# Two weight loads on ScalarE's DMA queue, one joined store at the end, and last outputs in the buffers of x

## The chip, the cores and the metric

The kernel runs on one core of a Trainium2 chip. The core has five engines that work beside each other, each through its own list of instructions in order: TensorE (PE, matrix products and transposes into PSUM), VectorE (DVE), ScalarE (ACT), GpSimd (POOL) and SyncE (SP), which here only issues transfers. Sixteen DMA engines move data between HBM and SBUF for all of them. A transfer that is issued on SyncE stands in SyncE's queue, one that is issued on ScalarE in ScalarE's queue. The metric is the device time of one execution in microseconds (us).

## What is computed

A gated linear recurrence over 6336 steps for 4 sequences of 256 channels, and a highway layer on its result:

```python
sig = 1.0 / (1.0 + np.exp(-f_logit))
f = lower_bound + (1.0 - lower_bound) * sig
i = 1.0 - f
for t in range(S):
    h = f[:, t] * h + i[:, t] * x[:, t]
    y[:, t] = h
...
H = np.maximum(y @ w_h, 0.0)
T = 1.0 / (1.0 + np.exp(-(y @ w_t + b_t)))
out = T * H + (1.0 - T) * y
```

`x` and `f_logit` are 26 MB each in float32, the output 26 MB, `w_h` and `w_t` 256 x 256 float32, 256 KB each.

## The kernel before

The 25344 rows (4 sequences of 6336) are cut into 21 units of 2 to 16 blocks of 128 rows (`parts`, line 43). The first two units and the last have 2 blocks, those in the middle 16 (two loads of 8). For a unit n the steps are, by their letters in the order table:

- l and x load logits and x (line 260, issued on SP), 8 KB for each partition in a full load; u is the sigmoid on ScalarE (272); b multiplies u and x, on GpSimd or VectorE (287).
- i and p transpose u and b into PSUM on TensorE (296, 321), so that channels lie on partitions and time runs along the row; f makes the decay from u on ScalarE or VectorE (311, 309).
- s is the recurrence, one scan instruction on VectorE for each half of the channels (330).
- z and g are the products with w_t and w_h on TensorE (343 and, for the same weights again, 148); t is the sigmoid of z on ScalarE (366), d the max on VectorE (373), e the product of d and t on GpSimd or VectorE (387).
- o adds y and e and transposes back to rows on TensorE (404, 405); c copies the result from PSUM to an SBUF buffer, on ScalarE (416) or VectorE (414); w stores that buffer (422, issued on SP).

Around the start stand once-only steps. `wh` and `wt` load the two weights into `w_raw` (207, 204). `WI` subtracts the identity from w_h on GpSimd (230). `WH` and `WT` scale the weights by one minus the lower bound into `w_sb`: WHv on VectorE (235), WT on ScalarE (237). The two parameter vectors `prm` of 1 KB each are loaded on ScalarE's queue (170, 171). k is a number of dummy matmuls on TensorE.

The order of all this work is written out by hand in the string `order` (lines 50 to 112). A token is a letter with unit, chunk and part, then the number of the buffer or PSUM bank after a colon, and a v at its name where VectorE takes the step instead of the engine named first. Each engine runs its instructions in the order of the tokens. What stands behind an instruction on its engine waits for it. Buffers are named by letter and number: `c20.0.1:3` writes into buffer o3, and waits until the store that last read o3 has ended. The last unit, number 20, has two blocks and is stored in two parts of one block each, so it has `o20.0.0`, `o20.0.1`, `c20.0.0v`, `c20.0.1`, `w20.0.0` and `w20.0.1`.

Of the kernel before, what the change touches and what calls it, by code (L numbers as in the profile page):

```python
# [11 lines left out]
FP32 = mybir.dt.float32  # L12
# [7 lines left out]
def kernel(  # L20
# [10 lines left out]
    nc = tc.nc  # L31
    B, S, D = x.shape
    assert (B, S, D) == (4, 6336, 256)
    P = 128
    NH = D // P
    NB = 8
# [3 lines left out]


    CHUNK, GROUP = {17: 4, 18: 4}, {17: 2, 18: 2, 19: 2, 20: 1}
    parts = [(2,), (2,), (4,), (8,), (8,), (8,), (8,), (8, 8), (8, 8), (8, 8), (8, 8), (8, 8), (8, 8), (8, 8), (8,), (8,), (8,), (8,), (8,), (4,), (2,)]
    units, at = [], 0
    for subs in parts:
# [2 lines left out]
    assert at == B * S  # L48

    order = """  # L50
k*4:0 l1.0:0 u1.0:0 i1.0.0:0 i1.0.1:1 l0.0:1 x0.0:0 x1.0:1 u0.0:1 b0.0.0:0 pc:2 wh i0.0.0:3 i0.0.1:4 WI k*1:5 cc
p0.0.0:2 p0.0.1:5 k*16:6 l2.0:2 u2.0:2 wt b1.0.0:1 p1.0.1:6 f1.0:0 dgv f0.0v:1 f0.1v:2 s0.1:0 x2.0:2 WHv s0.0:1
g0.0.1:0 p1.0.0:2 b2.0.1v:2 g0.0.0:3 WT z0.0.0:4 i2.0.1:5 f1.1:3 s1.1:2 z0.0.1:1 i2.0.0:6 d0.0.0:0 d0.0.1 b2.0.0
l3.0:3 f2.1v:1 k*4:7 p2.0.0:0 p2.0.1:3 s1.0:3 x3.0:3 z1.0.1:2 z1.0.0:5 g1.0.1:7 l4.0:4 t0.0.0:0 f2.0:2 t0.0.1 k*4:1
g1.0.0:1 e0.0.1 x4.0:4 u3.0:3 s2.0:4 i3.0.0:0 k*4:4 t1.0.0:1 t1.0.1 s2.1:5 g2.0.0:2 d1.0.1:1 b3.0.0:0 d1.0.0 d2.0.0:2
# [48 lines left out]
s18.1:3 c16.0.0:2 g17.0.1:0 i19.0.1:1 f19.1:1 b19.0.0 p19.0.1:2 d17.0.1:3 d17.0.0 z18.1.0:3 E17.1 e17.0.1 g18.1.0:4  # L104
o17.1.0:0 o17.1.1:1 z18.1.1:5 t18.1.0:2 d18.1.0:1 e18.1.0 g18.1.1:3 g18.0.1:4 z18.0.1:6 c17.1.0:1 w16.0.1 w16.0.0
s19.1:0 p19.0.0:0 w17.1.0 c17.1.1:0 e17.0.0v w17.1.1 t18.1.1 t18.0.1:0 o17.0.1:1 c17.0.1:3 d18.1.1 e18.1.1 s19.0:1
o17.0.0:2 c17.0.0:2 p20.0.1:3 z18.0.0:5 d18.0.1:0 t18.0.0 g18.0.0:1 o18.1.0:0 d18.0.0 c18.1.0:1 e18.0.1 w17.0.0
p20.0.0:2 s20.1:4 z19.0.0:4 t19.0.0:1 g19.0.0:5 e18.0.0 i20.0.0:0 f20.0:3 o18.1.1:1 c18.1.1:0 z19.0.1:3 d19.0.0:2
g19.0.1:0 t19.0.1 o18.0.1:4 c18.0.1:2 s20.0:5 z20.0.1:1 t20.0.1:2 e19.0.0 o18.0.0:2 w17.0.1 d19.0.1 w18.1.0 e19.0.1v
z20.0.0:0 t20.0.0 w18.1.1 c18.0.0v:3 g20.0.0:3 d20.0.0:3 w18.0.1 w18.0.0 o19.0.0:4 c19.0.0:1 w19.0.0 g20.0.1:1 d20.0.1  # L110
e20.0.0v o19.0.1:0 c19.0.1:0 w19.0.1 e20.0.1v o20.0.0:1 c20.0.0v:2 w20.0.0 o20.0.1:0 c20.0.1:3 w20.0.1
"""

    pool = ctx.enter_context(tc.tile_pool(name="sb", bufs=1))
# [3 lines left out]
    st = [dict() for _ in units]  # L118
    once = {}
    pin = tc.keep_in_program_order  # L120

    def sb(shape, dtype, name, slot=0):
        return pool.tile(shape, dtype, tag=f"{name}{slot}", name=name)
# [48 lines left out]
    cc = sb([P, NH], FP32, "cc")  # L172
    ncc = sb([P, NH], FP32, "ncc")
    bt = sb([P, NH], FP32, "bt")
    w_raw = sb([P, 2, NH, D], FP32, "w_raw")
# [12 lines left out]
    def chunk(n, q):  # L188

        nb, c = sum(units[n][1]), CHUNK.get(n, NB)  # L190
        return q * c, min(c, nb - q * c)
# [9 lines left out]
                mybir.DependencyClass.Sync, mybir.DependencyReason.DATA), reason="shared port")  # L201

    def do_wt(slot, eng):
        pin(nc.sync.dma_start(w_raw[:, 1], moe_w_t.rearrange("(h p) o -> p h o", p=P)))

    def do_wh(slot, eng):
        pin(nc.sync.dma_start(w_raw[:, 0], moe_w_h.rearrange("(h p) o -> p h o", p=P)))

    def do_pc(slot, eng):
        once["prmT"] = Banks(slot).one(0)[:, :2 * NH]  # L210
# [42 lines left out]
    def rows(full, at, j0, j1):  # L253
        return full[at + j0 * P:at + j1 * P, :].rearrange("(p j) d -> p j d", p=P)
# [104 lines left out]
    def half(n, q, name, h):  # L359
        M = chunk(n, q)[1] * P  # L360
        return st[n][name, q][:, h * M:(h + 1) * M]
# [27 lines left out]
    def blocks(n, q, r):  # L389
        c0, cl = chunk(n, q)  # L390
        g = GROUP.get(n, 4)
        return c0 + r * g, c0 + min(r * g + g, cl)

    def do_o(eng, slot, n, q, r):
        op = Banks(slot)
        j0, j1 = blocks(n, q, r)
        c0 = chunk(n, q)[0]
        g = j1 - j0
        for j in range(g):
            whole = slice(j0 * P + j, j0 * P + j + g * (P - 1) + 1, g)  # L400
            cols = slice((j0 - c0) * P + j, (j0 - c0) * P + j + g * (P - 1) + 1, g)
            for h in range(NH):
                o = op.part(j * D + h * P, j * D + (h + 1) * P)
                pin(nc.tensor.matmul(o, st[n]["y", h][:, whole], diag[:, h], start=True, stop=False))  # L404
                pin(nc.tensor.matmul(o, half(n, q, "d", h)[:, cols], ident_b, start=False, stop=True))  # L405
        st[n]["op", q, r] = op

    def do_c(eng, slot, n, q, r):
        j0, j1 = blocks(n, q, r)
        o = sb([P, 4 * D], FP32, "o", slot)  # L410
        op = st[n]["op", q, r].all((j1 - j0) * D)
        to = o[:, :(j1 - j0) * D]
        if eng:
            pin(nc.vector.tensor_copy(to, op))
        else:
            pin(nc.scalar.copy(to, op))  # L416
        st[n]["o", q, r] = o

    def do_w(eng, slot, n, q, r):
        j0, j1 = blocks(n, q, r)  # L420
        o = st[n]["o", q, r].rearrange("p (j d) -> p j d", d=D)
        pin(nc.sync.dma_start(rows(out, units[n][0], j0, j1), o[:, :j1 - j0]))

    here = locals()
    for token in order.split():
        token, _, slot = token.partition(":")
# [36 lines left out]
```

## Time and profile before

| | before |
|---|---|
| median of 3 runs | 208.44 us |
| lowest, highest | 208.13, 208.73 us |
| profiled execution, its own time | 209.02 us |
| its span in the profile | 206.9 us |
| HBM read, written | 52.43 MB, 25.95 MB |
| transfers from SP's queue, share of 16 engines' span | 94.1% |
| granted TensorE clock | full speed in all slices |

The span runs from the first to the last instruction that the profiler recorded; 2.1 us of the profiled execution lie outside. Rows of a timeline give start, duration, engine, line of the kernel, the operation with its output and inputs, and in brackets the idle time of that engine just before and what ended it. `x2` means that two instructions were merged into a row. SPq and ACTq are the issues of transfers, not the transfers.

### The profile page before, as it was taken

How to read it: one execution, taken by the hardware profiler on the slowest of the kernel's cores; microseconds unless marked ns; L12 is line 12 of the kernel's file. 1: busy time of each engine (PE TensorE's matmuls, PEld its weight loads, DVE VectorE, ACT ScalarE, POOL GpSimd, SP SyncE). 2: the span in 40 equal slices, each digit the busy share in tenths (PEclk: the TensorE clock that was granted, in tenths of full speed). 3: DMA queues.
4: the chain of work that ended last, by engine and by line, in shares of the span. 5: the costliest groups of instructions: out<-in, count | busy, mean ns of one | idle time of the engine just before them, and what ended most of it. 6: DMA issues, size and time to landing. Idle time of an engine off the chain costs nothing.

```text
span 206.9 us, 4654 instructions
## 1 busy us (share of the span) xinstructions
PE 194.4 (94%) x1850; PEld 135.4 (65%) x1850; DVE 193.8 (94%) x147; ACT 190.6 (92%) x182; POOL 173.8 (84%) x85
## 2 busy tenths in 40 slices
PE   7799999979989999999999999999999999999992
PEld 2365775745865757857757858657757868777770
DVE  0789999998999999999999999999999999999991
ACT  5178999989999999999999999999999999999982
POOL 3634695999999999979999869999899888999660
PEclk9999999999999999999999999999999999999999
DMA  6999999999999999999999999999999999853666
GB/s 187 380 425 423 417 420 421 412 413 427 417 421 429 412 421 417 421 413 428 421 394 426 427 413 416 424 423 418 417 411 414 334 394 345 353 222 146 251 245 213
DMA packets 16845, 78.68 MB, mean 380 GB/s; under 512 B 1844, under 2 KB 2616, under 8 KB 10936
## 3 DMA queue, kind: packets, MB, share of 16 engines
q1 hardware_dynamic: 16816, 78.39, 94.1%
q8 instruction: 14, 0.23, 0.4%
q14 instruction: 7, 0.06, 0.1%
q10 hardware_dynamic: 8, 0.00, 0.0%
HBM read 52.43 MB, written 25.95 MB: 379 GB/s over the span
## 4 chain that ended last, share of the span: by engine, by line
PE 50%; DVE 21%; DMA 12%; ACT 8%; issue 6%; SPq 1%; DVEq 0%; ACTq 0%
PE psum L343 16%; DVE y L330 13%; PE psum L148 11%; DMA l<-in_f_logit_dram 8%; PE psum L404 7%; DVE d L373 7%; PE psum L405 7%; PE psum L321 5%; ACT f L311 4%; PE psum L296 4%; DMA w_raw<-in_moe_w_h_dram 3%; ACT u L272 2%; ACT t L366 2%; DMA out_dram<-o 1%; SPq L260 1%
## 5 line engine op out<-in xcount | busy, mean ns | idle before, releaser
L287 POOL TENSOR_TENSOR bv<-u,x 128x1024 bf16<-128x1024 f16 (+2 forms) x39 | 101.4, 2613 | 19.7 <-DVE d L387 10.9
L330 DVE TENSOR_TENSOR_SCAN y<-f,y,psum 128x1024 bf16<-128x1024 f16 (+6 forms) x40 | 103.7, 2614 | 0.6 <-PE psum L404 0.3
L343 PE MATMUL psum<-y,w_sb 128*128 128x512 bf16 (+1 forms) x240 | 79.4, 368 | 4.1 <-ACT f L311 1.9
L387 POOL TENSOR_TENSOR d<-d,t 128x1024 bf16<-128x1024 bf16 (+3 forms) x33 | 71.3, 2173 | 5.7 <-ACT t L366 1.8
L373 DVE SCALAR_TENSOR_TENSOR d<-y,ncc,psum 128x1024 bf16<-128x1024 bf16 (+2 forms) x60 | 62.7, 1085 | 1.4 <-PE psum L148 0.5
L148 PE MATMUL psum<-y,w_sb 128*128 128x512 bf16 x168 | 63.6, 379 | 0.0
L366 ACT ACTIVATE t<-psum,bt 128x1024 bf16<-128x1024 f32 (+2 forms) x60 | 57.4, 988 | 1.7 <-PE psum L343 1.3
L272 ACT ACTIVATE u<-l 128x2048 f16<-128x2048 f32 (+2 forms) x28 | 48.1, 1743 | 6.0 <-DMA l<-in_f_logit_dram 5.9
L311 ACT ACTIVATE f<-psum,ncc 128x1024 f16<-128x1024 f16 (+3 forms) x38 | 50.3, 1344 | 0.7 <-PE psum L296 0.7
L416 ACT COPY o<-psum 128x1024 f32<-128x1024 f32 (+2 forms) x52 | 47.5, 945 | 3.3 <-DMA out_dram<-o 1.5
L404 PE MATMUL psum<-diag,y 128*128 128x128 f16 x396 | 49.8, 219 | 0.2
L405 PE MATMUL psum<-ident_b,d 128*128 128x128 bf16 x396 | 49.7, 219 | 0.0
L405 PEld LDWEIGHTS <-d 128*128 128x128 bf16 x396 | 43.5, 112 | 3.8 <-DVE d L387 0.4
L404 PEld LDWEIGHTS <-y 128*128 128x128 bf16 x396 | 43.6, 111 | 2.8
L343 PEld LDWEIGHTS <-w_sb 128*128 128x128 f16 x240 | 23.0, 98 | 19.5 <-issue 0.4
L321 PE MATMUL psum<-ident_f,bv 128*128 128x128 f32 x198 | 29.4, 275 | 2.0 <-DVE diag L222 1.2
L148 PEld LDWEIGHTS <-w_sb 128*128 128x128 f16 x168 | 16.4, 97 | 20.6 <-issue 6.4
L296 PE MATMUL psum<-ident_h,u 128*128 128x128 f16 x396 | 28.6, 220 | 1.0 <-ACT u L272 0.5
L296 PEld LDWEIGHTS <-u 128*128 128x128 f16 x396 | 24.9, 98 | 6.0 <-ACT u L272 1.3
L321 PEld LDWEIGHTS psum<-ident_f,bv 128*128 128x128 f32 x198 | 22.3, 141 | 7.0 <-POOL bv L287 1.5
L387 DVE TENSOR_TENSOR d<-d,t 128x1024 bf16<-128x1024 bf16 (+3 forms) x20 | 11.4, 598 | 0.1
L148 PE MATMUL psum<-zeros 128*128 128x512 bf16 x39 | 10.6, 398 | 0.0
(32 smaller groups left out, 40.6 us busy)
## 6 DMA issues: line engine op xcount, KB each, us to landing
l<-in_f_logit_dram SPq DMA_DIRECT2D x23, 1024.0 KB, 13.1
x<-in_x_dram SPq DMA_DIRECT2D x23, 1024.0 KB, 13.4
out_dram<-o SPq DMA_DIRECT2D x43, 512.0 KB, 8.1
out_dram<-o SPq DMA_DIRECT2D x12, 256.0 KB, 2.1
l<-in_f_logit_dram SPq DMA_DIRECT2D x2, 512.0 KB, 7.0
x<-in_x_dram SPq DMA_DIRECT2D x2, 512.0 KB, 7.3
l<-in_f_logit_dram SPq DMA_DIRECT2D x3, 256.0 KB, 2.9
x<-in_x_dram SPq DMA_DIRECT2D x3, 256.0 KB, 5.2
```

The costliest lines, as they stand in the source:

```text
L148: return pe.add_instruction(mybir.InstMatmult(name=nc.get_next_instruction_name(), start_tensor_calc=start, stop_tensor_calc=stop, tile_si ...
L287: shared(pin(e.tensor_mul(st[n]["bv", s][:, a:c].rearrange("p k d j -> p k j d"), st[n]["u", s][:, 2 * a:2 * c].rearrange("p (k j) d -> p ...
L296: pin(nc.tensor.transpose(uT[:, j * P:(j + 1) * P], st[n]["u", s][:, j, h * P:(h + 1) * P], ident_h))
L311: pin(nc.scalar.activation(to, of, AF.Identity, scale=ncc[:, h:h + 1], bias=1.0))
L321: pin(nc.tensor.transpose(words[:, k:k + g * (P - 1) + 1:g], pair, ident_f))
L330: pin(nc.vector.tensor_tensor_scan(y[:, c:e], st[n]["f", h][:, c:e], data, 0.0 if fresh else carry[h], op0=ALU.mult, op1=ALU.add))
L343: pin(nc.tensor.matmul(p.part(a, e), w, data, start=ki == 0, stop=ki == NH - 1))
L366: pin(nc.scalar.activation(half(n, q, "t", m), z, AF.Sigmoid, bias=bt[:, m:m + 1]))
L373: pin(nc.vector.scalar_tensor_tensor(half(n, q, "d", m), y, ncc[:, m:m + 1], g, op0=ALU.mult, op1=ALU.max))
L387: shared(pin(e.tensor_mul(d, d, t)), not eng)
L404: pin(nc.tensor.matmul(o, st[n]["y", h][:, whole], diag[:, h], start=True, stop=False))
L405: pin(nc.tensor.matmul(o, half(n, q, "d", h)[:, cols], ident_b, start=False, stop=True))
```

## The change

It has three parts. The two weight loads are issued on ScalarE instead of SP, and stand behind ScalarE's first two u (tokens `whv wtv`). Unit 20 is still copied in two halves, but into one buffer, and stored by one transfer of 256 KB where there were two of 128 KB; the columns of its matmuls are taken so that a partition's two rows are neighbours in the output. The outputs of units 18, 19 and 20 are copied into the buffers of x, which no load uses any more at that time, instead of the four buffers o0 to o3.

```diff
+    JOINED, FROM_X = (20,), (18, 19, 20)
...
-... b0.0.0:0 pc:2 wh i0.0.0:3 i0.0.1:4 WI k*1:5 cc p0.0.0:2 p0.0.1:5 k*16:6 l2.0:2 u2.0:2 wt b1.0.0:1 ...
+... b0.0.0:0 pc:2 i0.0.0:3 i0.0.1:4 k*1:5 cc p0.0.0:2 p0.0.1:5 k*16:6 l2.0:2 whv wtv WI u2.0:2 b1.0.0:1 ...
...
-e20.0.0v o19.0.1:0 c19.0.1:0 w19.0.1 e20.0.1v o20.0.0:1 c20.0.0v:2 w20.0.0 o20.0.1:0 c20.0.1:3 w20.0.1
+e20.0.0v o19.0.1:0 c19.0.1:0 w19.0.1 e20.0.1v o20.0.0:1 c20.0.0v:4 o20.0.1:0 c20.0.1 w20.0.0
...
     def do_wt(slot, eng):
-        pin(nc.sync.dma_start(w_raw[:, 1], moe_w_t.rearrange("(h p) o -> p h o", p=P)))
+        pin((nc.scalar if eng else nc.sync).dma_start(w_raw[:, 1], moe_w_t.rearrange("(h p) o -> p h o", p=P)))
...
     def do_wh(slot, eng):
-        pin(nc.sync.dma_start(w_raw[:, 0], moe_w_h.rearrange("(h p) o -> p h o", p=P)))
+        pin((nc.scalar if eng else nc.sync).dma_start(w_raw[:, 0], moe_w_h.rearrange("(h p) o -> p h o", p=P)))
...
     def do_o(eng, slot, n, q, r):
         op = Banks(slot)
         j0, j1 = blocks(n, q, r)
-        c0 = chunk(n, q)[0]
-        g = j1 - j0
-        for j in range(g):
+        c0, cl = chunk(n, q)
+        js, g = range(j1 - j0), j1 - j0
+        if n in JOINED:
+            j0, js, g = c0, range(j0 - c0, j1 - c0), cl
+        for at, j in enumerate(js):
             whole = slice(j0 * P + j, j0 * P + j + g * (P - 1) + 1, g)
             cols = slice((j0 - c0) * P + j, (j0 - c0) * P + j + g * (P - 1) + 1, g)
             for h in range(NH):
-                o = op.part(j * D + h * P, j * D + (h + 1) * P)
+                o = op.part(at * D + h * P, at * D + (h + 1) * P)
...
     def do_c(eng, slot, n, q, r):
         j0, j1 = blocks(n, q, r)
-        o = sb([P, 4 * D], FP32, "o", slot)
+        a, r0 = 0, r
+        if n in JOINED:
+            a, r0 = (j0 - chunk(n, q)[0]) * D, 0
+        if ("o", q, r0) not in st[n]:
+            if n in FROM_X:
+                o = sb([P, NB, D], FP32, "x", slot).rearrange("p j d -> p (j d)")
+            else:
+                o = sb([P, 4 * D], FP32, "o", slot)
+            st[n]["o", q, r0] = o
         op = st[n]["op", q, r].all((j1 - j0) * D)
-        to = o[:, :(j1 - j0) * D]
+        to = st[n]["o", q, r0][:, a:a + (j1 - j0) * D]
...
     def do_w(eng, slot, n, q, r):
         j0, j1 = blocks(n, q, r)
+        if n in JOINED:
+            j0, j1 = chunk(n, q)[0], sum(chunk(n, q))
```

The instructions of TensorE, VectorE and GpSimd keep their order; three places move on ScalarE and SP. The start of ScalarE's list before (prm are the parameter vectors, u and f the steps of the first units, w_sb the scaled weight w_t):

```order
L170 DMA prm<-in_lower_bound_dram 2x128
L171 DMA prm<-in_moe_b_t_dram 2x128
L272 ACTIVATE u<-l 128x512 x2
L272 ACTIVATE u<-l 128x1024
L311 ACTIVATE f<-psum,ncc 128x256
L237 ACTIVATE w_sb<-w_raw,cc 128x256 x2
```

and with the change:

```order
L171 DMA prm<-in_lower_bound_dram 2x128
L172 DMA prm<-in_moe_b_t_dram 2x128
L273 ACTIVATE u<-l 128x512 x2
L208 DMA w_raw<-in_moe_w_h_dram 128x2x256
L205 DMA w_raw<-in_moe_w_t_dram 128x2x256
L273 ACTIVATE u<-l 128x1024
L312 ACTIVATE f<-psum,ncc 128x256
L238 ACTIVATE w_sb<-w_raw,cc 128x256 x2
```

The two loads of the weights now stand between the u of units 1 and 0 and the u of unit 2. The start of SP's list before, with the loads of units 1 and 0 first:

```order
L260 DMA l<-in_f_logit_dram 128x512 x2
L260 DMA x<-in_x_dram 128x512 x2
L207 DMA w_raw<-in_moe_w_h_dram 128x2x256
L260 DMA l<-in_f_logit_dram 128x1024
L204 DMA w_raw<-in_moe_w_t_dram 128x2x256
L260 DMA x<-in_x_dram 128x1024
L260 DMA l<-in_f_logit_dram 128x2048
```

and with the change:

```order
L261 DMA l<-in_f_logit_dram 128x512 x2
L261 DMA x<-in_x_dram 128x512 x2
L261 DMA l<-in_f_logit_dram 128x1024
L261 DMA x<-in_x_dram 128x1024
L261 DMA l<-in_f_logit_dram 128x2048
```

The loads of unit 2 (128x1024) and all behind them have moved up by one and by two places. The end of SP's list before, with the buffers' numbers (each o is a copy's output; the last three are units 19 and 20):

```order
L422 DMA out_0_dram<-o_2720 128x512
L422 DMA out_0_dram<-o_2736 128x512
L422 DMA out_0_dram<-o_2751 128x512
L422 DMA out_0_dram<-o_2759 128x256
L422 DMA out_0_dram<-o_2766 128x256
```

and with the change:

```order
L434 DMA out_0_dram<-x_2695 128x512
L434 DMA out_0_dram<-x_2720 128x512
L434 DMA out_0_dram<-x_2736 128x512
L434 DMA out_0_dram<-x_2751 128x512
L434 DMA out_0_dram<-x_2759 128x512
```

The two stores of half a unit have become one store of the whole, behind both copies.

More of the change, by code (lines that the diff above doesn't have):

```diff
@@ L50 @@
     order = """
-k*4:0 l1.0:0 u1.0:0 i1.0.0:0 i1.0.1:1 l0.0:1 x0.0:0 x1.0:1 u0.0:1 b0.0.0:0 pc:2 wh i0.0.0:3 i0.0.1:4 WI k*1:5 cc
-p0.0.0:2 p0.0.1:5 k*16:6 l2.0:2 u2.0:2 wt b1.0.0:1 p1.0.1:6 f1.0:0 dgv f0.0v:1 f0.1v:2 s0.1:0 x2.0:2 WHv s0.0:1
+k*4:0 l1.0:0 u1.0:0 i1.0.0:0 i1.0.1:1 l0.0:1 x0.0:0 x1.0:1 u0.0:1 b0.0.0:0 pc:2 i0.0.0:3 i0.0.1:4 k*1:5 cc p0.0.0:2
+p0.0.1:5 k*16:6 l2.0:2 whv wtv WI u2.0:2 b1.0.0:1 p1.0.1:6 f1.0:0 dgv f0.0v:1 f0.1v:2 s0.1:0 x2.0:2 WHv s0.0:1
 g0.0.1:0 p1.0.0:2 b2.0.1v:2 g0.0.0:3 WT z0.0.0:4 i2.0.1:5 f1.1:3 s1.1:2 z0.0.1:1 i2.0.0:6 d0.0.0:0 d0.0.1 b2.0.0
@@ L106 @@
 s19.1:0 p19.0.0:0 w17.1.0 c17.1.1:0 e17.0.0v w17.1.1 t18.1.1 t18.0.1:0 o17.0.1:1 c17.0.1:3 d18.1.1 e18.1.1 s19.0:1
[L107 to L110, printed above, removed]
-e20.0.0v o19.0.1:0 c19.0.1:0 w19.0.1 e20.0.1v o20.0.0:1 c20.0.0v:2 w20.0.0 o20.0.1:0 c20.0.1:3 w20.0.1
+o17.0.0:2 c17.0.0:2 p20.0.1:3 z18.0.0:5 d18.0.1:0 t18.0.0 g18.0.0:1 o18.1.0:0 d18.0.0 c18.1.0:0 e18.0.1 w17.0.0
+p20.0.0:2 s20.1:4 z19.0.0:4 t19.0.0:1 g19.0.0:5 e18.0.0 i20.0.0:0 f20.0:3 o18.1.1:1 c18.1.1:4 z19.0.1:3 d19.0.0:2
+g19.0.1:0 t19.0.1 o18.0.1:4 c18.0.1:1 s20.0:5 z20.0.1:1 t20.0.1:2 e19.0.0 o18.0.0:2 w17.0.1 d19.0.1 w18.1.0 e19.0.1v
+z20.0.0:0 t20.0.0 w18.1.1 c18.0.0v:3 g20.0.0:3 d20.0.0:3 w18.0.1 w18.0.0 o19.0.0:4 c19.0.0:2 w19.0.0 g20.0.1:1 d20.0.1
+e20.0.0v o19.0.1:0 c19.0.1:0 w19.0.1 e20.0.1v o20.0.0:1 c20.0.0v:4 o20.0.1:0 c20.0.1 w20.0.0
 """
@@ L416, in do_c @@
             pin(nc.scalar.copy(to, op))
-        st[n]["o", q, r] = o
     def do_w(eng, slot, n, q, r):
         j0, j1 = blocks(n, q, r)
+        if n in JOINED:
+            j0, j1 = chunk(n, q)[0], sum(chunk(n, q))
         o = st[n]["o", q, r].rearrange("p (j d) -> p j d", d=D)
```

## The prediction

> **What bounds the kernel now.** I read the page first, then the chain of waits, then the timeline of each engine at the two places that the change touches: the first 28 us and the last 5 us.
>
> ```profile
> span 206.9 us, 4654 instructions
> PE 194.4 (94%) x1850; PEld 135.4 (65%) x1850; DVE 193.8 (94%) x147; ACT 190.6 (92%) x182; POOL 173.8 (84%) x85
> DMA  6999999999999999999999999999999999853666
> ```
>
> TensorE, VectorE and ScalarE are each busy for more than nine tenths of the span, and the DMA engines are full until slice 34. Nobody has spare time in the middle, so a shift of the start or of the end is all that a change of a few transfers can bring. The chain of waits, asked for the first 40 us, says what holds the start:
>
> ```profile
> 2.59 5.41 DMA w_raw<-in_moe_w_h_dram
> 8.08 16.64 DMA l<-in_f_logit_dram
> ```
>
> The load of w_h lands at 8.00 and frees the semaphore on which SP issues l of unit 5; that load lands at 8.08 + 16.64 = 24.72, and ScalarE turns it into u at 24.80 (row below). The load did not need 16.64 us of its own: it stood in a full queue. Its landing is set by the bytes ahead of it, and those are the same bytes after the change.
>
> The timeline of ScalarE in that stretch (start, duration, engine, line; in brackets the idle time ahead and what ended it):
>
> ```profile
> 3.48 1.38 ACT L272 ACTIVATE u<-l 128x512 f16<-128x512 f32 x2 [0.65 <-DMA l<-in_f_logit_dram]
> 9.33 1.06 ACT L272 ACTIVATE u<-l 128x1024 f16<-128x1024 f32 x1 [4.47 <-DMA l<-in_f_logit_dram]
> 10.65 0.90 ACT L237 ACTIVATE w_sb<-w_raw,cc 128x256 f16<-128x256 f32 x2
> 11.45 0.46 ACT L311 ACTIVATE f<-psum,ncc 128x256 f16<-128x256 f16 x1
> 18.91 1.91 ACT L272 ACTIVATE u<-l 128x2048 f16<-128x2048 f32 x1 [0.46 <-DMA l<-in_f_logit_dram]
> 24.80 1.91 ACT L272 ACTIVATE u<-l 128x2048 f16<-128x2048 f32 x1 [0.34 <-DMA l<-in_f_logit_dram]
> ```
>
> Twice, at 18.91 and 24.80, ScalarE has caught up with the loads and waits. Work that is early before those points gains nothing; work that is late by less than the waits costs little. VectorE and TensorE have such gaps as well:
>
> ```profile
> 9.44 1.03 DVE L235 TENSOR_SCALAR w_sb<-w_raw,cc 128x256 f16<-128x256 f32 x2
> 10.39 0.67 DVE L330 TENSOR_TENSOR_SCAN y<-f,psum 128x256 bf16<-128x256 f16 x1
> 11.45 0.74 DVE L287 TENSOR_TENSOR bv<-u,x 128x512 bf16<-128x512 f16 x1 [0.39 <-DMA x<-in_x_dram]
> 12.08 0.73 DVE L330 TENSOR_TENSOR_SCAN y<-f,y,psum 128x256 bf16<-128x256 f16 x1
> ...
> 11.69 0.27 PE L321 MATMUL psum<-ident_f,bv 128*128 128x128 f32 x1
> 14.95 0.82 PE L343 MATMUL psum<-y,w_sb 128*128 128x256 bf16 x6 [0.26 <-DVE y L330]
> 26.77 0.62 PE L296 MATMUL psum<-ident_h,u 128*128 128x128 f16 x8 [0.23 <-ACT u L272]
> ```
>
> VectorE has waited 0.39 us for x of unit 2 by 11.45, and TensorE has 0.26 + 0.23 = 0.49 us of idle time between 12 and 27 us.
>
> **The change part by part: the weights.** Two issues leave SP's queue and stand on ScalarE behind its first two u, which end at 3.48 + 1.38 = 4.86. Before, SP issued w_h at 2.59 and w_t 1 us later. What the two issues cost ScalarE: between 0.43 us each (SP's own price for w_h) and 1.17 us (the dearest early issue of SP). Twice 1.17 ends at 7.2, and ScalarE's next instruction waits for its data until 9.33. The wait of 4.47 us covers the issues whichever price holds, so they cost nothing; without that cover they would be 0.9 to 2.3 us.
>
> ```profile
> 2.59 0.43 SPq L207 DMA_DIRECT2D w_raw<-in_moe_w_h_dram  x1
> 4.06 1.17 SPq L260 DMA_DIRECT2D x<-in_x_dram  x1
> 8.07 0.87 POOL L230 TENSOR_TENSOR w_raw<-w_raw,ident_f 128x128 f32<-128x128 f32 x2 [0.17 <-DMA w_raw<-in_moe_w_h_dram]
> 8.90 1.17 POOL L287 TENSOR_TENSOR bv<-u,x 128x512 bf16<-128x512 f16 x1
> ```
>
> What matters is when w_h and w_t land. The trace has no large transfer on ScalarE's queue, but it has two small ones: prm, 1 KB each. The rows of the issues, and then those of the DMA queues for 1.6 to 1.7 us, for 2.0 to 2.6 us, and for 2.7 to 3.0 us (q1 is SP's queue, q10 ScalarE's; packets, MB, share of 16 engines):
>
> ```profile
> 0.73 0.53 ACTq L170 DMA_DIRECT2D prm<-in_lower_bound_dram  x1
> 1.35 0.24 ACTq L171 DMA_DIRECT2D prm<-in_moe_b_t_dram  x1
> ...
> 0.73 0.86 SPq L260 DMA_DIRECT2D l<-in_f_logit_dram  x2
> ...
> q10 hardware_dynamic: 4, 0.00, 4.2%
> ...
> DMA packets 56, 0.11 MB, mean 191 GB/s; under 512 B 0, under 2 KB 0, under 8 KB 56
> q1 hardware_dynamic: 56, 0.11, 73.3%
> ...
> DMA packets 67, 0.11 MB, mean 352 GB/s; under 512 B 14, under 2 KB 16, under 8 KB 67
> q10 hardware_dynamic: 4, 0.00, 4.5%
> ```
>
> The first prm met empty engines and moved 0.9 us after its issue. The second, issued at 1.35, would by that have moved at 2.25, but no packet of q10 is among those of 2.0 to 2.6; all four come in 2.7 to 3.0. There the first packets under 512 B of SP's queue appear as well, which I take for those that close its first load (it is used from 3.48 on). SP had issued two loads by 0.73 + 0.86 = 1.59, the second about when prm was issued; prm did not wait for that one. So a transfer on ScalarE's queue neither stands behind all that SP has issued nor shares each engine piece by piece: it waited for the load under way and then had its turn.
>
> The Trainium skill, page "DMA: Bandwidth & Descriptors", section "Queues, rings and completion order", says that a DMA engine takes turns between its rings, a whole packet of typically 9 to 17 descriptors at a time. By that rule w_h waits for at most the one load that is under way, which is the case that I sum below.
>
> In that case the order on an engine is at worst l of unit 2, w_h, x of unit 2, w_t, where before it was w_h, l, w_t, x. The pairs hold the same bytes, so w_h lands between 8.00 (as now) and 9.33, when l of unit 2 had landed behind it; w_t lands between its use at 10.65 and 11.45, when x of unit 2 had landed behind it.
>
> The late end, worked through: GpSimd's subtraction (0.87 us) runs 9.4 to 10.3 instead of 8.07 to 8.94, and b of unit 1 behind it ends at 11.4 instead of 10.07; TensorE, which fills its time with dummy matmuls, asks for that only at 11.69. VectorE's scaling of w_h starts at 10.3 instead of 9.44, the scan behind it ends at about 11.9, and of that 0.39 us is the wait for x at 11.45 that was there anyway. ScalarE's scaling of w_t starts at 11.45 instead of 10.65, its f behind it ends at 12.7 instead of 11.91, and the scan at 12.08, which needs this f, starts at 12.75: 0.67 us late. TensorE's 0.49 us of gaps then takes most of it: 0.67 - 0.49 = 0.18 us is left at 28 us. The early end is no loss and no gain, since the loads at 18.91 and 24.80 land when they did. I take +0.1 us, the middle between 0 (landing as now) and 0.18 (landing latest, gaps usable); bounds 0 and +0.67.
>
> **The end.** The last three outputs before the end:
>
> ```profile
> 202.60 0.42 DVE L414 COPY o<-psum 128x256 f32<-128x256 f32 x1 [0.32 <-PE psum L405]
> 202.69 0.22 PE L405 MATMUL psum<-ident_b,d 128*128 128x128 bf16 x1
> 203.28 0.37 ACT L416 COPY o<-psum 128x256 f32<-128x256 f32 x1 [0.81 <-DMA out_dram<-o]
> 203.05 0.96 SPq L422 DMA_DIRECT2D out_dram<-o  x2
> out_dram<-o SPq DMA_DIRECT2D x8, 256.0 KB, 2.0
> out_dram<-o SPq DMA_DIRECT2D x2, 128.0 KB, 2.0
> 203.00:204.00 1.00, 0.00 (x0) 0.00 (x0) 0.03 (x1) 0.37 (x1) 0.00 (x0) 1.00 1.04 385
> 204.00:205.00 1.00, 0.00 (x0) 0.00 (x0) 0.00 (x0) 0.00 (x0) 0.00 (x0) 1.00 0.86 285
> ```
>
> ScalarE's last copy shows 0.81 us of waiting for a store, because its buffer o3 was still being written out. But its data were ready only when the matmul of 202.69 ended, at 202.91; a few hundredths later, at about 202.95, the copy starts in a free buffer. So the wait that goes is 203.28 - 202.95 = 0.33 us, not 0.81. The last store is then issued at 202.95 + 0.37 + 0.03 = 203.35 instead of 203.28 + 0.37 + 0.03 = 203.68 (the 0.03 is from VectorE's copy, done at 203.02, to SP's issue at 203.05). What does it give? By the time from issue to landing, 2.0 us for 256 KB as for 128 KB, the full -0.33. But the DMA engines' share is 1.04 and 0.86 in the last two microseconds: the stores queue for the engines, and 256 KB at 385 GB/s take 0.68 us. With 0.85 us from issue to the first byte (about the 0.9 of prm) the joined store moves from 204.2 to 204.9, where the engines now run dry at about 205.0: -0.1. The first half, which goes out at 203.05 now, leaves 0.3 us later. I take -0.15, nearer to the engines' end than to the landings; bounds -0.33 and +0.1, the latter if the late first half costs more than the fewer, larger pieces save.
>
> The Trainium skill, same page, section "Anatomy of one DMA — SWDGE (gpsimd) path", gives a store a fixed 2.0 us and bytes at 436 GB/s beside it, for another path than this one. By it 256 KB would take 0.3 us longer than 128 KB and the end would gain 0.03 us; the rows' equal 2.0 us speak against so large a difference.
>
> The other outputs that move to buffers of x had no wait for a buffer: the list of waits of the last 12 us has the 0.81 alone. The last readers of those buffers are GpSimd's products, and they end at 187.01 + 2.32 = 189.33, before the first of these copies in the order, so nothing is gained or lost there.
>
> ```profile
> 187.01 2.32 POOL L287 TENSOR_TENSOR bv<-u,x 128x512 bf16<-128x512 f16 x2
> ```
>
> The strided columns of unit 20's last matmuls change no count of matmuls.
>
> Sum, on the profiled execution of 209.02 us (span 206.9 and 2.1 outside): +0.10 - 0.15 = -0.05, that is 208.97. The median of the runs, 208.44, is 0.58 lower, so the same difference gives 208.4.
>
> **Rivals.** First, **turns piece by piece** (slower): each engine alternates single pieces of the two queues. By their shapes w_h has 256 rows of 1 KB, 16 on each of 16 engines, and l and x of unit 2 have 128 rows of 4 KB each, 8 on an engine, so w_h lands with x, at 11.45, and w_t with x of unit 3. GpSimd shows when that is:
>
> ```profile
> 16.49 2.14 POOL L287 TENSOR_TENSOR bv<-u,x 128x1024 bf16<-128x1024 f16 x1 [1.27 <-DMA x<-in_x_dram]
> ```
>
> ScalarE stands at the scaling of w_t until 16.49 instead of 10.65, with f, t and u behind it, and VectorE's scan of 12.08 starts at 16.49 + 0.90 + 0.46 = 17.85, 5.8 us late. TensorE's gaps take 0.5 of it: +5.3, less 0.15 at the end, or 213.6. It decides as soon as w_t lands more than about 1 us after 10.65. The packets of prm speak against it. Chance 0.10.
>
> Second, **the late end, not absorbed** (slower): w_t at 11.45 and TensorE's gaps not usable, since VectorE's late scans come just where it waits for them: +0.67 at the start, 0 at the end: 209.1, and a little over where the store is later too. Half of it lies above the bound of 0.3%. Chance 0.18.
>
> Third, **both ends gain** (faster): x of unit 2, now ahead of w_t, lands early enough to end VectorE's wait of 0.39 us at 11.45, the gain is carried on, and the last store gives its whole 0.33: -0.72, or 207.7. It decides from the loads: l of unit 5 would have to land earlier too. Against it stand ScalarE's waits at 18.91 and 24.80, which end with loads whose bytes ahead have not changed. Chance 0.14.
>
> **How the numbers follow.** Forecast (no change but for tenths of a us): 0.58; rivals 0.10, 0.18 and 0.14. A measurement of this kernel tells about 0.3%, 0.6 us, from no change. Slower by more: 0.10 + half of 0.18 + 0.04 of the forecast's edge = 0.23. Faster by more: most of the third rival, 0.11, and 0.04 of the forecast's other edge: 0.15. Same: 0.62. The likeliest case alone spans 207.9 to 208.9; with the second and third it is 207.5 to 209.8, which leaves out the first rival and little else.
>
> **What would show it.** Right: the subtraction on GpSimd starts between 8.0 and 9.4, the scaling on ScalarE between 10.6 and 11.5, u of unit 5 at 24.8 within 0.3, the last copy on ScalarE has no wait for a store and the last store is issued near 0.3 us earlier relative to TensorE's last matmul, while the engines run dry 0 to 0.2 us earlier. Wrong: w_t landing past 12, a gap of more than 1 us on ScalarE ahead of it, l of unit 5 landing at another time than 24.7 by over half a us, or a middle that takes another time between two like points although no instruction in it changed.

## The result, and the profile after

| | before | after |
|---|---|---|
| median | 208.28 us (6 runs) | 218.56 us (6 runs) |
| lowest, highest | 207.99, 208.73 us | 217.69, 218.95 us |
| profiled execution, and its span | 209.02, 206.9 us | 217.97, 216.2 us |
| mean granted TensorE clock | 1.000 | 0.976 |

The ratio after / before is 1.0485, with a 95% interval of 1.0459 to 1.0511. The kernel is slower by about 10 us, far outside the predicted range. Here and below a median is that of all runs, and a ratio leaves out the few runs in a slower state of the chip (one of e3, one of e7, one of before beside e1 to e4).

The profile page of the changed kernel, the rows that answer to those shown of before and the two DMA queues (packets, MB, share of 16 engines; q1 is SP's queue, q10 ScalarE's):

```profile
span 216.2 us, 4646 instructions
PE 196.8 (91%) x1850; PEld 136.2 (63%) x1850; DVE 193.4 (89%) x147; ACT 190.6 (88%) x182; POOL 173.7 (80%) x85
PEclk9995699999999999999999999999999999999999
DMA  6999999997889999999999999999999999854756
q1 hardware_dynamic: 16128, 77.86, 91.4%
q10 hardware_dynamic: 552, 0.53, 0.7%
```

Busy times are those of before to within 2.4 us. So the span grew by waiting, not by work. Before, q10 had 8 packets; two times 256 rows of 1 KB are most of the 544 that came on top.

The chain of waits of the first 40 us (start, duration, what) now runs through one transfer that was not on it:

```profile
1.17 3.13 DMA l<-in_f_logit_dram
4.32 0.44 ACT u L273
4.80 15.96 DMA w_raw<-in_moe_w_t_dram
20.85 0.52 ACT w_sb L238
```

The load of w_t takes 15.96 us from issue to landing, for 256 KB, and ScalarE's scaling follows at once. The timelines of ScalarE, GpSimd, VectorE and SP in the same stretch:

```profile
4.33 0.43 ACTq L208 DMA_DIRECT2D w_raw<-in_moe_w_h_dram  x1
4.80 0.48 ACTq L205 DMA_DIRECT2D w_raw<-in_moe_w_t_dram  x1
8.35 1.06 ACT L273 ACTIVATE u<-l 128x1024 f16<-128x1024 f32 x1 [3.40 <-DMA l<-in_f_logit_dram]
20.85 0.91 ACT L238 ACTIVATE w_sb<-w_raw,cc 128x256 f16<-128x256 f32 x2 [11.08 <-DMA w_raw<-in_moe_w_t_dram]
...
15.40 0.86 POOL L231 TENSOR_TENSOR w_raw<-w_raw,ident_f 128x128 f32<-128x128 f32 x2 [8.96 <-DMA w_raw<-in_moe_w_h_dram]
...
22.15 0.75 DVE L331 TENSOR_TENSOR_SCAN y<-f,y,psum 128x256 bf16<-128x256 f16 x1 [3.35 <-ACT f L312]
38.35 2.34 DVE L331 TENSOR_TENSOR_SCAN y<-f,y,psum 128x1024 bf16<-128x1024 f16 x1
...
8.41 0.33 SPq L261 DMA_DIRECT2D l<-in_f_logit_dram  x1
15.40 0.33 SPq L261 DMA_DIRECT2D x<-in_x_dram  x1
20.83 0.33 SPq L261 DMA_DIRECT2D l<-in_f_logit_dram  x1
```

GpSimd gets w_h at 15.40 instead of 8.07 and stands idle for 8.96 us. ScalarE gets w_t at 20.85 instead of 10.65, with 11.08 us idle. VectorE's scan that needs the f behind that scaling starts at 22.15, where before it started at 12.08: 10.07 us late. At the third scan of 1024 columns the distance is 38.35 - 27.92 = 10.43 us (the row of before is in the fence below), and at the last matmul 212.18 - 202.69 = 9.49. So the loss is made in the first 22 us and carried to the end. Nothing later makes it much larger or takes much of it back.

```profile
27.92 2.35 DVE L330 TENSOR_TENSOR_SCAN y<-f,y,psum 128x1024 bf16<-128x1024 f16 x1 [0.16 <-ACT f L311]
```

Where do 256 KB spend 11 and 16 us? The rows of the DMA queues of the changed kernel for 5 to 8 us, 9 to 10 us, 17 to 18 us, and 20 to 21 us:

```profile
DMA packets 318, 1.10 MB, mean 367 GB/s; under 512 B 39, under 2 KB 39, under 8 KB 311
q1 hardware_dynamic: 318, 1.10, 103.2%
...
q1 hardware_dynamic: 48, 0.38, 91.7%
q10 hardware_dynamic: 44, 0.05, 12.7%
...
q1 hardware_dynamic: 46, 0.36, 87.9%
q10 hardware_dynamic: 45, 0.05, 13.5%
...
q1 hardware_dynamic: 53, 0.42, 100.5%
q10 hardware_dynamic: 1, 0.00, 0.1%
```

From 5 to 8 us not one packet of ScalarE's queue moves, though w_h was issued at 4.33. From 8 us on the queues move 44 packets against 48, and 45 against 46. SP's pieces are 0.38 MB / 48 = 8 KB, ScalarE's are 1 KB. So the weights get 0.05 of 0.43 MB in a microsecond. After 20 us, when w_t is in, the weights' queue is empty again.

Equal counts alone would also fit turns of eight pieces against eight. The order of the single packets in the trace decides it. From 9 to 19 us 474 pieces of 1 KB moved. In the last 4 ns of such a piece a piece of 8 KB starts 522 times, where the stretches of 4 ns around have 49 to 119 starts; another piece of 1 KB starts 89 times, where the stretches around have 67 to 119. In the last 4 ns of the 446 pieces of 8 KB a piece of 1 KB starts 505 times (35 to 113 around), one of 8 KB 94 times (40 to 115 around). So the engines moved one piece of one queue, then one of the other.

### The profile page after: what moved, and what is told of

It is laid out like the page before. It is cut to its first block, busy times and chain, and to the rows that moved or that the text cites. A ratio compares the mean times of both kernels' runs of the same rounds, so it can differ in the third digit from the quotient of the medians.

```text
span 216.2 us, 4646 instructions
## 1 busy us (share of the span) xinstructions
PE 196.8 (91%) x1850; PEld 136.2 (63%) x1850; DVE 193.4 (89%) x147; ACT 190.6 (88%) x182; POOL 173.7 (80%) x85
## 4 chain that ended last, share of the span: by engine, by line
PE 56%; DVE 22%; DMA 9%; issue 6%; ACT 6%; SPq 0%; DVEq 0%; ACTq 0%
PE psum L344 17%; DVE y L331 14%; PE psum L149 13%; DVE d L374 8%; DMA w_raw<-in_moe_w_t_dram 7%; PE psum L407 7%; PE psum L408 7%; PE psum L322 6%; PE psum L297 5%; ACT f L312 3%; DMA l<-in_f_logit_dram 1%; ACT u L273 1%; ACT t L367 1%; PE psum L250 1%; ACT o L427 1%
## 5 line engine op out<-in xcount | busy, mean ns | idle before, releaser
L344 PE MATMUL psum<-y,w_sb 128*128 128x512 bf16 (+1 forms) x240 | 80.8, 373 | 5.4 <-ACT w_sb L238 1.9
L427 ACT COPY o<-psum 128x1024 f32<-128x1024 f32 (+1 forms) x46 | 44.3, 997 | 1.2 <-ACT f L312 0.6
L322 PE MATMUL psum<-ident_f,bv 128*128 128x128 f32 x198 | 30.0, 278 | 8.2 <-POOL bv L288 7.3
## 6 DMA issues: line engine op xcount, KB each, us to landing
l<-in_f_logit_dram SPq DMA_DIRECT2D x23, 1024.0 KB, 10.1
x<-in_x_dram SPq DMA_DIRECT2D x23, 1024.0 KB, 10.1
```

Of the source, the lines that this page charges most:

```text
L322: pin(nc.tensor.transpose(words[:, k:k + g * (P - 1) + 1:g], pair, ident_f))
L344: pin(nc.tensor.matmul(p.part(a, e), w, data, start=ki == 0, stop=ki == NH - 1))
```

## The experiments

Eleven kernels were run. Their edits are given against the changed kernel or against before. The reading that the trace of after suggests (the theory of the expectations): a load on ScalarE's queue first waits for what SP issued ahead of it, then gets one piece for each piece of SP's, whatever their sizes. The rivals are a lower granted clock, a stall of ScalarE by its issues, and the changed end.

**e1, the end alone.** The changed kernel with both weights back in SP's queue at their old places in the order.

```diff
-p0.0.1:5 k*16:6 l2.0:2 whv wtv WI u2.0:2 b1.0.0:1
+... pc:2 wh i0.0.0:3 i0.0.1:4 WI ... k*16:6 l2.0:2 u2.0:2 wt b1.0.0:1
```

> The change with both weight loads back on SP, at their places of before; the joined store and the buffers of x stay. Theory (the late weights are the whole loss): no loss is left, time 207.9 to 208.3, the store worth 0 to -0.3 us against before. Rival (the end of the change costs as well, by the late first half or the copies in buffers of x): above 208.9.

207.25 us, ratio 0.9974 (0.9951 to 0.9997), granted clock 1.0. The end does not make the loss; it gains a little, more than was expected.

**e2, the weights alone.** Before, with only the two loads on ScalarE's queue (`whv wtv` and the two lines of `do_wh` and `do_wt`).

```diff
-... pc:2 wh i0.0.0:3 i0.0.1:4 WI ... k*16:6 l2.0:2 u2.0:2 wt b1.0.0:1
+p0.0.1:5 k*16:6 l2.0:2 whv wtv WI u2.0:2 b1.0.0:1
```

> The kernel before with nothing but the weight loads moved, as the change moves them. Theory: the whole loss, 218.3 to 219.0, w_h landing near 15.4 us and w_t near 20.8. Rival (half of the loss from the end): 213 to 216.

218.0 us, ratio 1.0465 (1.0407 to 1.0522). That is 0.3 us below what was expected. The scan that started at 12.08 starts at 21.97:

```profile
21.97 0.75 DVE L330 TENSOR_TENSOR_SCAN y<-f,y,psum 128x256 bf16<-128x256 f16 x1 [3.48 <-ACT f L311]
```

With e1 this puts the whole loss on the weights.

**e3, the weights first.** The changed kernel with both issues ahead of ScalarE's first u, at 1.65 and 2.12 us instead of 4.33 and 4.80.

```diff
-k*4:0 l1.0:0 ... l2.0:2 whv wtv WI u2.0:2
+whv wtv k*4:0 l1.0:0 ... l2.0:2 WI u2.0:2
```

> The change with both weight loads still on ScalarE's queue but issued ahead of the first u, right behind prm, near 1.6 and 2.2 us. Theory (the DMA engines take one piece of each queue in turn, behind what SP had issued before): the weights then alternate with pieces of 2 and 4 KB, w_h lands near 7.5 and w_t near 10 us, time 207.7 to 208.8. Rival (ScalarE's queue gets a fixed small share of the engines, about 47 GB/s as measured, whatever the pieces): 256 KB take 5.6 us each, w_t lands near 14, time 211 to 213.

208.05 us, ratio 0.9999 (0.9965 to 1.0032), the time of before. Against e1 it is 0.25% more by the ratios, 0.5 us, but their intervals overlap. The rows of q1 and q10 for 4 to 5 us and for 6 to 7 us:

```profile
q1 hardware_dynamic: 88, 0.15, 50.0%
q10 hardware_dynamic: 142, 0.14, 44.8%
...
q1 hardware_dynamic: 76, 0.24, 65.7%
q10 hardware_dynamic: 139, 0.13, 40.1%
```

And ScalarE's and VectorE's timeline:

```profile
12.70 0.91 ACT L238 ACTIVATE w_sb<-w_raw,cc 128x256 f16<-128x256 f32 x2 [1.42 <-DMA w_raw<-in_moe_w_t_dram]
14.00 0.75 DVE L331 TENSOR_TENSOR_SCAN y<-f,y,psum 128x256 bf16<-128x256 f16 x1 [1.50 <-ACT f L312]
```

Here the weights meet the loads of the first units, whose pieces are small (0.15 MB in 88 packets, 1.7 KB each on average), and get about half of the bytes from 4 to 5 us. With 142 packets against 88, and 139 against 76, they have more than one piece for each of SP's, although the two queues together keep the engines busy (50.0 + 44.8% and 65.7 + 40.1%). So one piece for one is not what this run shows; why it differs beside small pieces stays open. The landings are later than was expected (w_h for GpSimd at 9.08), but 8 us earlier for w_t than in the changed kernel. So ScalarE's queue as such is not slow, and its share is no fixed one. It depends on what it meets.

**e4, pieces of 2 KB.** The changed kernel, where each partition reads two neighbouring rows of a weight: 128 pieces of 2 KB where there were 256 of 1 KB. The rows of the weights stand in another order then, so the output is another; the work is the same.

```diff
-moe_w_t.rearrange("(h p) o -> p h o", p=P)
+moe_w_t.rearrange("(p h) o -> p h o", p=P)
-moe_w_h.rearrange("(h p) o -> p h o", p=P)
+moe_w_h.rearrange("(p h) o -> p h o", p=P)
```

> The change with the weights read in 128 pieces of 2 KB where there were 256 of 1 KB (each partition takes two neighbouring rows, so the weights are permuted and the output is another). Theory (one piece in turn): half the turns, w_h lands near 12.9 and w_t near 16 us, time 212.5 to 214.5. Rival (a fixed share in bytes): both land as in the change, 15.4 and 20.8, time 218 to 219.

212.97 us, ratio 1.0228 (1.0163 to 1.0293). The queues' rows for 9 to 10 us:

```profile
q1 hardware_dynamic: 41, 0.34, 84.2%
q10 hardware_dynamic: 40, 0.08, 21.2%
```

And the timeline of GpSimd and ScalarE, when the weights are used:

```profile
11.87 0.86 POOL L231 TENSOR_TENSOR w_raw<-w_raw,ident_f 128x128 f32<-128x128 f32 x2 [4.90 <-DMA w_raw<-in_moe_w_h_dram]
15.05 0.91 ACT L238 ACTIVATE w_sb<-w_raw,cc 128x256 f16<-128x256 f32 x2 [5.83 <-DMA w_raw<-in_moe_w_t_dram]
```

Still one piece for one, 41 and 40, but each carries 2 KB. From w_h to w_t it is 15.05 - 11.87 = 3.18 us instead of 20.85 - 15.40 = 5.45. Worked out as one for one, 128 pieces of 2 KB and 128 of 8 KB are 1.31 MB, at 418 GB/s 3.1 us. Both weights land about 1 us earlier than was expected. Same bytes, same queue, same place in the order, half the pieces, and about half the loss. Beside pieces of 8 KB, the number of pieces counts, and not the bytes.

**e5, TensorE kept warm.** The changed kernel with 39 more dummy matmuls where TensorE waits.

```diff
-k*16:6 l2.0:2 whv wtv ... WT z0.0.0:4
+k*46:6 l2.0:2 whv wtv ... WT k*9:4 z0.0.0:4
```

> The change with 30 more dummy matmuls ahead of the transpose that waits for GpSimd and 9 more ahead of the first product with w_t, so that TensorE does not idle while the weights are awaited (in the change it idled 7 and 2 us there, and its granted clock then showed 0.5 for some 6 us). Theory (late weights alone, the clock costs little because VectorE's delay was 10.1 us at the first scan behind w_t and 10.4 us after the clock was back): granted clock 1.0, time 217.8 to 218.6. Rival (the lower clock is a good part of the loss): 215 to 217.

218.0 us, ratio 1.0485 (1.0447 to 1.0524), as without them. The windows of 6 us (window, length, busy time with instructions in brackets for PE, PEld, DVE, ACT and POOL, granted clock, DMA share, GB/s), of the changed kernel and then of e5:

```profile
12.00:18.00 6.00, 0.47 (x1) 0.18 (x1) 2.11 (x3) 0.00 (x0) 2.03 (x3) 0.77 1.01 409
18.00:24.00 6.00, 3.83 (x19) 2.29 (x20) 2.65 (x6) 2.17 (x5) 1.16 (x1) 0.50 1.02 418
24.00:30.00 6.00, 6.00 (x37) 3.63 (x36) 4.74 (x7) 5.09 (x7) 2.81 (x2) 0.87 1.02 425
```

```profile
12.00:18.00 6.00, 5.53 (x27) 2.51 (x27) 2.56 (x4) 0.00 (x0) 2.04 (x3) 1.00 1.03 416
18.00:24.00 6.00, 4.88 (x33) 2.71 (x32) 2.56 (x6) 2.73 (x7) 1.16 (x1) 1.00 1.01 416
24.00:30.00 6.00, 5.55 (x37) 3.18 (x37) 5.41 (x7) 5.54 (x7) 2.81 (x2) 1.00 1.02 419
```

The clock falls to 0.50 in the changed kernel and stays at 1.00 in e5, and the time is the same within the intervals of about 0.4%. So the low clock, which came with the wait, is not the loss. In the trace e5 is 38.35 - 37.31 = 1.04 us ahead at the third scan of 1024 columns, of which 0.36 was there at the first scan behind w_t; none of it is left in the median that the intervals could tell.

**e6, late in one queue.** Both weights in SP's queue, but w_h behind the loads of units 2 and 3 and w_t behind l of unit 4, so that they land late without a second queue. The loads named in the new line are taken out of their later places.

```diff
-l2.0:2 whv wtv WI u2.0:2
+l2.0:2 x2.0:2 l3.0:3 x3.0:3 wh l4.0:4 wt x4.0:4 WI u2.0:2
```

> The change with both weights on SP's queue, but late in it: w_h behind x of unit 3, w_t behind l of unit 4. By the bytes ahead of them w_h lands near 15.8 and w_t near 18.7 us. Theory (only the time at which w_t lands counts, not which queue it is on): the scaling of w_t starts 8.1 us later than before, time 215 to 216.5. Rival (a second queue costs something of its own, in the transfers of SP beside it): below 213.

215.04 us, ratio 1.0333 (1.0299 to 1.0366). GpSimd has w_h at 15.51, ScalarE w_t at 18.77, and the scan starts at 20.07, 7.99 us late:

```profile
20.07 0.75 DVE L331 TENSOR_TENSOR_SCAN y<-f,y,psum 128x256 bf16<-128x256 f16 x1 [1.16 <-ACT f L312]
```

So lateness alone, without a second queue, costs 6.9 us (6.2 to 7.6). That is most of what the changed kernel would lose by such a lateness (10.1 us for 10.07). Whether sharing the engines adds the rest, about 1 us, is not shown.

**e7, w_t alone.** e1 with only w_t on ScalarE's queue.

```diff
-l2.0:2 u2.0:2 wt b1.0.0:1
+l2.0:2 wtv u2.0:2 b1.0.0:1
```

> The change with w_h back on SP at its place of before, and only w_t on ScalarE's queue behind the first two u. Theory (behind what SP has issued, then one piece in turn): 16 pieces on each engine against 16 of 4 and 8 KB, w_t lands near 15.3, its scaling starts 4.7 us late, time 211.8 to 213.2. Rival (w_h's lateness is what counts, through GpSimd and TensorE): below 209.5.

212.36 us, ratio 1.0192 (1.0151 to 1.0233). The scan starts 4.06 us late, at 16.14:

```profile
14.85 0.91 ACT L238 ACTIVATE w_sb<-w_raw,cc 128x256 f16<-128x256 f32 x2 [4.74 <-DMA w_raw<-in_moe_w_t_dram]
16.14 0.75 DVE L331 TENSOR_TENSOR_SCAN y<-f,y,psum 128x256 bf16<-128x256 f16 x1 [5.16 <-ACT f L312]
```

One weight instead of two in the second queue, and less than half of the loss. The w_t of the changed kernel stands behind w_h in the same queue and waits for its turns too.

The six kernels with the weights late, by when the scan that started at 12.08 starts:

| | scan at | late by | ratio to before |
|---|---|---|---|
| e3 | 14.00 | 1.92 us | 0.9999 |
| e7 | 16.14 | 4.06 us | 1.0192 (+4.0 us) |
| e4 | 16.34 | 4.26 us | 1.0228 (+4.7 us) |
| e6 | 20.07 | 7.99 us | 1.0333 (+6.9 us) |
| e2 | 21.97 | 9.89 us | 1.0465 (+9.7 us) |
| after | 22.15 | 10.07 us | 1.0485 (+10.1 us) |

The us in brackets are the ratio's excess times the median of before in the same runs. All but e2 hold the end's gain of some 0.5 us as well. From 4 us on the loss is the whole lateness, to within about 1 us; at 1.92 us no loss against before shows.

**e8 to e11, the end.** With the weights as before: e8 joins the last store and leaves all outputs in o buffers; e9 has the buffers of x for units 18 to 20 and two half stores; e10 has them for unit 20 alone, e11 for units 18 and 19 alone, both with two half stores. The buffer numbers in the order are set to fit.

```diff
 e8
-JOINED, FROM_X = (20,), (18, 19, 20)
+JOINED, FROM_X = (20,), ()
 e9
+JOINED, FROM_X = (), (18, 19, 20)
 e10
+JOINED, FROM_X = (), (20,)
 e11
+JOINED, FROM_X = (), (18, 19)
```

> The end of the change without the buffers of x: weights on SP as before, the last unit copied in halves into one of the buffers o and stored whole, the copies of units 18 to 20 in the buffers o as before. Theory (what is gained is the wait of the last copy for a buffer, since with one buffer for both halves the second copy needs no other): the last copy starts 0.3 us earlier behind the last matmul, 207.4 to 207.8 where before is 208.0. Rival (the gain comes from the free buffers of x): no gain, 207.9 to 208.2.

> The end of the change without the joined store: weights on SP as before, copies of units 18 to 20 in buffers of x, the last unit stored in two transfers of 128 KB. Theory (the wait of the last copy is the gain, and the DMA engines then take as long for two halves as for the whole): 207.4 to 207.8, the last copy without a wait for a store. Rival (the joined store, with fewer and larger pieces, is the gain): no gain, 207.9 to 208.2.

> The weights and all copies as before, but for the two outputs of unit 20, which go to buffers of x; two half stores. If the gain of the x buffers (e9, ratio 0.9964) is the last copy's wait for a store that is taken away, this has all of it: ratio 0.9960 to 0.9984 (the wait was 0.33 us, 0.16%), and the last copy waits only for TensorE. If the gain comes from the outputs of units 18 and 19, which stay in the four o buffers here, this has none: 0.999 to 1.001.

> The weights as before; the outputs of units 18 and 19 go to buffers of x, those of unit 20 to o2 and o3 as before (which are free then, since c18.0.0 no longer uses o3 right ahead of them); two half stores. The last copy's wait for a store is gone here too, so by the first theory (the wait) the ratio is that of e10, 0.9960 to 0.9984. By the second (the outputs of units 18 and 19 make the gain) it is that of e9, 0.9964, and e10 is 1.000. If it matters that the last stores themselves read buffers of x, this has none, 0.999 to 1.001, and e10 has all.

| | ratio to before | last copy starts | last matmul to end of span |
|---|---|---|---|
| before | | 0.59 us after the last matmul | 4.21 us |
| e1 (joined, x) | 0.9974 (0.9951 to 0.9997) | 0.30 us | 3.81 us |
| e8 (joined, o) | 1.0002 (0.9980 to 1.0023) | 0.30 us | 4.86 us |
| e9 (halves, x) | 0.9964 (0.9944 to 0.9985) | 0.30 us | 3.58 us |
| e10 (halves, x for 20) | 0.9997 (0.9978 to 1.0016) | 0.26 us | 3.84 us |
| e11 (halves, x for 18, 19) | 0.9984 (0.9962 to 1.0006) | 0.26 us | 3.63 us |

The last two columns come from one profiled execution each (starts of the last matmul and of ScalarE's last copy). Rows of e9 as an example:

```profile
202.62 0.22 PE L408 MATMUL psum<-ident_b,d 128*128 128x128 bf16 x1
202.92 0.37 ACT L427 COPY x<-psum 128x256 f32<-128x256 f32 x1 [0.52 <-PE psum L408]
```

All five take away the last copy's wait for a store, and all five start that copy 0.3 us earlier relative to the last matmul. Yet only e1 and e9 are faster than before beyond their intervals, and e8 shows no gain, against what its first theory expected. In e8's profiled execution one DMA engine was still writing after the others had ended: the DMA share is 0.42 in the one microsecond, and 0.03 in the next, half a microsecond of one engine in 16, which is the last with data (the columns are those of the windows above).

```profile
203.20:204.20 1.00, 0.00 (x0) 0.00 (x0) 0.00 (x0) 0.00 (x0) 0.00 (x0) 1.00 0.42 156
204.20:205.20 1.00, 0.00 (x0) 0.00 (x0) 0.00 (x0) 0.00 (x0) 0.00 (x0) 1.00 0.03 10
```

What the gain comes from stays open. By the first theory e10 should have had all of it, and it has none that shows; e11 lies between; but the intervals of e9, e10 and e11 overlap. What holds is a gain with the buffers of x for all three units, 0.26% in e1 and 0.36% in e9, and that the joined store adds nothing to it that shows (e8 against before, e1 against e9). The best versions are e9 (207.35 us, ratio 0.9964) and e1 (207.25 us, 0.9974), which can't be told apart; both are faster than before and than the changed kernel.

## Why the prediction was wrong

**What bounds the kernel: right.** All that the change did happened in the first 22 us and the last 5 us, and the middle carried it along.

**The issues on ScalarE: right.** They end at 5.28, and ScalarE waits until 8.35 for its next data anyway.

**The landing of the weights: wrong, and this is the step that failed.** The prediction read the packets of prm as "it waited for the load under way and then had its turn", and so put w_h at 8.00 to 9.33 and w_t at 10.65 to 11.45. They were used at 15.40 and 20.85. The reading went wrong in two ways. First, w_h did not wait for one load: from its issue at 4.33 until 8 us no packet of q10 moved, while SP's l and x of unit 2, issued at 2.58 and 3.37, were moved (u of unit 2 starts at 8.35); it began together with l of unit 3, which SP had issued at 4.32 like it. Second, "its turn" was one piece and not the whole load. The four packets of that prm, two rows of 512 B and two of 4 B, are too few to tell these apart: a load of one or two pieces has its whole turn in one or two. The quoted rows also fit a prm that waits behind the load issued before it and then moves piece by piece beside the second of the two. The page of the Trainium skill that the prediction leaned on ("DMA: Bandwidth & Descriptors", section "Queues, rings and completion order") has the engines take whole packets, 9 to 17 descriptors typically, in turn. By that the 16 pieces that w_h has on each engine would be through in one or two turns. The trace disagrees, with 44 packets against 48 in a microsecond that follow each other one by one, and e4 disagrees, where half the pieces took 3.18 us instead of 5.45: beside pieces of 8 KB a turn was one piece.

**The late end of the start: right in its chain, wrong in its size.** The scan does follow the landing of w_t as worked out (20.85 + 0.90 + 0.46 = 22.21, measured 22.15). The 0.67 us of the sum was 10.07. The 0.49 us that TensorE's gaps were to take is too small to be seen at this size. In e3 the scan is 2.37 us later than in e1 (14.00 against 11.63) and the ratios differ by 0.5 us, so some of a small lateness may be taken up; with intervals that overlap this is not shown.

**The loads behind: half right.** That l of unit 5 is set by the bytes ahead of it did not matter, as ScalarE had not the weights. But the semaphores were named and not followed: SP's issues at 15.40 and 20.83 now wait for w_h and w_t. The engines did not run dry then (409 to 425 GB/s from 12 to 30 us). They did later: from 42 to 60 us they moved 331 GB/s, where before it was 419. The row of before, then two of the changed kernel:

```profile
42.00:60.00 18.00, 15.62 (x162) 11.43 (x163) 17.27 (x10) 17.29 (x14) 18.00 (x6) 1.00 1.02 419
...
42.00:60.00 18.00, 16.58 (x140) 10.53 (x138) 18.00 (x12) 18.00 (x16) 16.26 (x7) 1.00 0.88 331
60.00:80.00 20.00, 18.09 (x192) 13.52 (x190) 19.92 (x12) 20.00 (x16) 20.00 (x7) 1.00 0.95 360
```

VectorE and ScalarE are busy nearly throughout these two windows, so the thin transfers there should follow from buffers that come free late and not be a second loss. That is argued from the windows and not shown; e6, with one queue, has a smaller dip of the kind (381 GB/s from 42 to 60 us).

**The end: right about the copy, its gain not traced to that.** The wait is gone: the copy starts 0.30 us after the last matmul instead of 0.59. Taken was -0.15 us with bounds of -0.33 and +0.1. e1 measured 0.26% less, 0.54 us, with an interval of 0.06 to 1.0 us, which the taken value and the better bound both lie in. But e8 and e10 lose the same wait and show no gain, so the runs do not show that the gain is this wait, and the joined store, which the sum counted on, adds nothing that shows.

**The first rival** had the mechanism, and a chance of 0.10, because "the packets of prm speak against it". Its price of 5.3 us was half of the 10.1 measured. It let w_h start with l of unit 2 and share with pieces of 4 KB. In fact w_h started one pair of loads further on and shared with pieces of 8 KB. Worked out with those: 256 pieces of 1 KB and 256 of 8 KB are 2.36 MB, at 418 GB/s 5.6 us for each weight; from w_h to w_t it was 5.45. From about 8 us two such stretches end at 19.3. Among the packets of the trace the last piece of w_t starts at 19.96, and w_t landed at 4.80 + 15.96 = 20.76. That is the 10 us lost.

## What to carry to other kernels

A small load of many short rows did badly in a second queue beside long rows: with 1 KB and 2 KB against 8 KB each of its pieces paid for one of the other queue's, so its time followed the number of its pieces and not its bytes. Two things helped here: issuing it before the long loads (e3) and making its pieces longer (e4). And a pattern read off a transfer of two pieces says little about one of 256.

## What the runs showed that was not expected

- Two queues shared the DMA engines one piece for one: 44 and 48, 45 and 46 packets in a microsecond with 1 KB against 8 KB, 40 and 41 with 2 KB. A load of 256 KB took 15.96 us to land. Beside pieces of 2 and 4 KB, in e3, it was not one for one (142 against 88).
- The second queue did not start beside transfers that the first had issued before: 3.7 us without a packet in the changed kernel, from 4.33 to 8.03 us. By then all 512 pieces of the loads of units 0 and 1 and 239 of the 256 of unit 2 had started. In e3 the weights, issued at 1.65, began at 3.69, when 273 of those 512 had. What makes a load wait for the earlier ones of the other queue stays open.
- TensorE's granted clock fell to 0.50 from 18 to 24 us after some 6 us with almost no matmul. Filling that with dummy matmuls held it at 1.00 and changed the time by nothing that can be measured (both ratios 1.0485).
- Taking a visible wait of 0.3 us off the last copy went with a gain of between 0 and 0.36% in five kernels that all did it. At this size the profile of a single execution and the median do not agree on where a tenth of a per cent is.
